# Listing an expert's tokens: the place split as 64 a + b, and two token columns to one loaded matrix

## Chip, cores and metric

One Trainium2 chip, one of its cores. The metric is the device time of one execution in microseconds; the lower the better. The kernel before takes 1235.56 us (median of three runs).

## What is computed

The reference transforms x in two dimensions, routes the rows through a first mixture of experts in which every expert takes exactly N / 8 tokens, and then through a second one without a limit:

```python
X = np.fft.fft(np.fft.fft(x, axis=1), axis=2).real         # x: [4, 2496, 256]
x = X.reshape(9984, 256)
logits = x @ w_gate                                        # first mixture, 8 experts, cap = 1248
for idx in np.argsort(-logits.flatten()):
    tok, e = idx // 8, idx % 8
    if assigned[tok] < 0 and counts[e] < cap:
        assigned[tok] = e; counts[e] += 1
out[assigned == e] = np.maximum(x[assigned == e] @ w1[e], 0) @ w2[e]        # F = 1024
# second mixture: e = argmax of out @ w_gate; gate * sigmoid(out @ w_output_gate)[e] * ffn_e(out)
```

The change is in the first mixture, between the choice of an expert's tokens and the gathering of their rows. There the device has, for each of the 9984 tokens (kept as 128 partitions by 80 columns), its place in the expert's list, a number from 0 to 1247, or a very large one for the tokens of other experts. Wanted is the inverse: for each place the token that stands there.

## The kernel before, in words

The program has three stages. `Fft.over_d` and `Fft.rows` (L139, L361) transform x and write the rows to the DRAM tensor xd, up to some 150 us. Then `Moe1` runs the first mixture expert by expert up to some 760 us, and `Moe2` the second. `Moe1.ffn` (L949) makes an expert's products: `ffn1_unit` (L781) multiplies the gathered and transposed rows with w1, ScalarE and VectorE split the relu into two float16 halves (L861, L867), and `ffn2_unit` (L789) multiplies them with w2.

Beside these products runs the choice of the next experts. `Select.phase` (L540) searches for the threshold at which an expert is full (`counts`, L502: a mask on VectorE, L512, ten small matmuls, L517, one more, L534) and computes each token's place (L605 to L629): two counts on TensorE (L607), a small copy ct on VectorE (L609) after which the flow yields 0.6, and products that need ct (L613, L614). `Select.places(k)` (L631) then lists expert k's tokens. `Moe1.prepare` (L998) calls it for the experts 1 to 7 and `Select.run` (L462) for expert 0; the gather of the rows from xd (L830) reads the list, idx.

The listing splits a place as 128 t + b. For a column c of 128 tokens, hb[:, :, c] is the one-hot matrix of b (128 by 128) and ha[:, :, :, c] holds, for the ten values of t, one-hot times c and one-hot times the partition p. The product of the two, summed over the 80 columns, has at (b, t) the column and the partition of the token with that place. So hb is the loaded matrix (the weights) of 80 matmuls (L658), and ha streams 20 columns past each of them. VectorE builds hb in four tiles of 20 columns each (L652), for 2 buffers, and ha in three steps (hx L643, L645, L646). nf (L660) and idx (L661) read the sum px.

```python
            for c in range(HB):
                cc = q * HB + c
                nc.tensor.matmul(px[:, :20], hb[:, :, c], ha[:, :, :, cc], start=(cc == 0), stop=(cc == 79))
```

In hb the column is the innermost index, so the 128 weights of one column lie HB = 20 numbers apart.

What sets the order: `Flow` (L1095) runs the side work as generators. Each yield gives the number of microseconds, by the flow's own count, after which the next piece is emitted between two units of the main products; `issue_after` keeps a piece behind the unit before it. The framework's scheduler then orders each engine's queue by these priorities. All queues are run in order on the chip, so an instruction of the listing that waits on TensorE also holds the expert's products behind it.

The constants come in two pieces: ch (tri, tric, ioa, ci, one; loaded at L1452) and iob, which `later` (L473) loads apart.

Of the kernel before, what the change touches and what calls it, by code (L numbers as in the profile page):

```python
# [10 lines left out]
F32 = mybir.dt.float32  # L11
# [3 lines left out]
OP = mybir.AluOpType  # L15
# [11 lines left out]
QW = 138  # 128 of q, q = 128, 8 experts, padding  # L27
# [7 lines left out]
def seq_rows():  # L35
    """[parity, 640]: the even and the odd positions up to the middle"""
    s = 2 * np.arange(640)[None] + np.arange(2)[:, None]
    return np.where(s <= H, s, -1)


def tables():
    # over the sequence: [parity, block of k, position, (cos, sin), block of positions, half, k]
# [6 lines left out]
    # over d: [d, half, (cos, sin), q]  # L49
# [9 lines left out]
    # for the gate: [q, block of q, (cos, sin, alternating), half, d]  # L59
# [7 lines left out]
    # the row d = 128: 16 (-1)^q, and what makes its halves' rows  # L67
# [8 lines left out]
def row_tokens():  # L76
    """the token of each internal row: [batch, (k, S - k, H - k, H + k), k]"""
# [10 lines left out]
def row_columns():  # L88
    """the order of q in a row of X"""
    return np.concatenate([np.arange(129), np.arange(255, 128, -1)])  # L90


def lay_x(x):
# [5 lines left out]
    # [parity, batch, d, ((d, s), (d, S - s), (256 - d, S - s), (256 - d, s)), position]  # L99
    xa = xa.transpose(4, 0, 1, 2, 3, 5).copy()  # L100
    xa[:, :, :, 1] = xa[:, :, :, 1, ::-1].copy()
    # [(half of the batches, (s, S - s), 3 copies), parity, batch, position]
# [23 lines left out]
class Fft:  # L126
    """Re(fft2(x)): first over d, with the gate's logits as further columns, then over the sequence."""
# [11 lines left out]
    def over_d(self, io, wk):  # L139
        """the columns' halves y"""  # L140
# [10 lines left out]
        def busy(n):  # L151
            """keeps TensorE's clock up while it waits"""
            for _ in range(n):
                nc.tensor.matmul(pw, one[:, :128], one, start=True, stop=True)
# [28 lines left out]
        # the gate's columns  # L183
# [16 lines left out]
        # the row d = 128: halves (hi, lo, hi) against (hi, hi, lo)  # L200
# [99 lines left out]
    def products(self, dst, k, par, cs, bs, qs, fine=False):  # L300
        """the sum over the positions of a parity; in three steps"""
# [11 lines left out]
    def logit_sums(self, par):  # L313
        """a parity's share of the logits, and of the column q = 128"""
# [15 lines left out]
    def logits(self):  # L330
        """the logits of all rows, and the column q = 128"""
# [8 lines left out]
    def half_rows(self, k, par, bs, fine=False):  # L340
        """a parity's share of a block of k: the differences and the sums of its cos and sin parts"""
# [19 lines left out]
    def rows(self, wk, k, bs):  # L361
        """a block of k: its rows of X"""
# [26 lines left out]

HK = ()  # L390
HQ = (1, 3)
# [14 lines left out]
def sel_consts():  # L406
# [20 lines left out]
    h["ioa"] = np.broadcast_to(np.arange(10)[:, None], (128, 10, 80)).reshape(128, -1)  # L427
    h["ci"] = np.broadcast_to(np.arange(80), (128, 80))
    h["one"] = np.ones((128, 128))
    h["iob"] = np.broadcast_to(np.arange(128)[:, None], (128, 128, HB)).reshape(128, -1)  # L430
# [8 lines left out]
class Select:  # L439
# [22 lines left out]
    def run(self):  # L462
        """fills expert after expert"""
# [9 lines left out]
    def later(self, pool, ch):  # L473
        """what only places needs"""
# [27 lines left out]
    def counts(self, lo, tt, n):  # L502
        """the mask m of the tokens with value - lo at or over each of n thresholds, and
        -> the experts' counts, [128, (expert, threshold)]"""
# [35 lines left out]
    def phase(self, k):  # L540
# [4 lines left out]
        # the first of the best experts  # L545
# [25 lines left out]
        # the bracket [lo, hi)  # L571
# [13 lines left out]
        # the expert that is full first  # L585
# [11 lines left out]
        # its tokens: those at or over hi, and the first of the bracket  # L597
# [24 lines left out]
        # the next phase's values  # L622
# [8 lines left out]
    def places(self, k):  # L631
# [4 lines left out]
        nc.vector.tensor_single_scalar(pi[:, 1], pi[:, 0], 7, op=OP.logical_shift_right)  # L636
        nc.vector.tensor_single_scalar(pi[:, 2], pi[:, 0], 127, op=OP.bitwise_and)
# [3 lines left out]
        ha = w.tile([128, 2, 10, 80], F16, name="ha", bufs=1)  # L641
        hx = w.tile([128, 10, 80], F16, name="hx", bufs=1)
        nc.vector.tensor_tensor(hx, h["ioa"].rearrange("p (a c) -> p a c", a=10),  # L643
                                pa[:, 0, None, :].to_broadcast([128, 10, 80]), op=OP.is_equal)
        nc.vector.tensor_mul(ha[:, 0], hx, h["ci"][:, None, :].to_broadcast([128, 10, 80]))  # L645
        nc.vector.tensor_scalar(ha[:, 1], hx, f["pi"], None, op0=OP.mult)  # L646
        wait = 6.0
        px = self.psum.tile([128, 512], F32, name="px", bufs=1)
        iob = self.iob.rearrange("p (b c) -> p b c", c=HB)
        for q in range(80 // HB):  # L650
            hb = w.tile([128, 128, HB], F16, name="hb")
            (nc.gpsimd if k in HK and q in HQ else nc.vector).tensor_tensor(hb, iob, pa[:, 1, None, q * HB:(q + 1) * HB].to_broadcast([128, 128, HB]),  # L652
                                    op=OP.is_equal)
            yield wait
            wait = 1.5
            for c in range(HB):
                cc = q * HB + c
                nc.tensor.matmul(px[:, :20], hb[:, :, c], ha[:, :, :, cc], start=(cc == 0), stop=(cc == 79))  # L658
        nf = w.tile([128, 20], F32, name="nf")
# [37 lines left out]
class Weights:  # L697
    """An expert's float32 matrices, loaded and split into halves: [:, part, half], the parts w1's two
    blocks of rows and w2's two fours of blocks."""
# [20 lines left out]
    def split(self, fs, quick, step=512):  # L720
        """-> the halves (w1's, and w2's with room for w2 wg beside it), and the steps that make them"""
# [23 lines left out]
    def gate(self, w2, fs, wg, psum, quick):  # L745
        """w2 wg beside w2, in steps"""
# [46 lines left out]
class Moe1:  # L793
# [15 lines left out]
    def gate_consts(self):  # L809
        """halves of both gates' matrices"""  # L810
# [24 lines left out]
    def xt(self, xg, c):  # L835
        """transposed halves of a chunk's rows, and the steps that make them"""
# [44 lines left out]
    def route(self, yr, k):  # L881
        """expert, scale and place of an expert's 1248 rows"""
# [615 lines left out]
```

## Time and profile before

| | |
|---|---|
| Three runs | 1234.17, 1235.56, 1239.19 us |
| Median | 1235.56 us |
| Profiled execution, from first to last instruction (its own time: the record gives the span alone) | 1230.4 us |
| TensorE busy with matmuls | 1153.9 us, 94% |
| VectorE busy | 758.1 us, 62% |
| GpSimd busy | 519.8 us, 42% |
| ScalarE busy | 450.3 us, 37% |
| Mean granted clock of TensorE | 0.975 |

PE is TensorE, PEld its loading of weights (which overlaps PE), DVE VectorE, ACT ScalarE, POOL GpSimd, SP the engine whose queue issues most DMAs. Busy time is time with at least one instruction of the engine under way. Matmuls are pipelined: one lasts some 0.2 us from start to end, but the next starts much sooner, so the cost of a batch is read from the distance between starts, and the last one's end is modelled. The clock is given as a share of 2.4 GHz and has two levels, 1.2 and 2.4 GHz. In the views, an entry in brackets is the engine's idle time before the instruction and what ended it.

### The profile page before, as it was taken

The numbers are of one execution on the slowest core, as the hardware profiler recorded it, in microseconds if no ns is written. First come the engines' busy times: TensorE is split into PE (matmuls) and PEld (weight loads), VectorE is DVE, ScalarE is ACT, GpSimd is POOL, SyncE is SP. The second block draws the span as 40 slices with busy tenths as digits, with TensorE's granted clock in tenths as the row PEclk, the third lists the DMA queues.
The fourth block names the chain that finished last, engine by engine and source line by source line (L and its number), as shares of the span: only waits on it lengthen the run. The fifth ranks groups of instructions, "written<-read, shape, count | busy, mean of one in ns | idle before, by whom it ended". The sixth has DMA issues, their size and how long they took to land. (4 is left out here: it accounts for less than half of the span.)

```text
span 1230.4 us, 25668 instructions
## 1 busy us (share of the span) xinstructions
PE 1153.9 (94%) x10286; PEld 844.6 (69%) x10286; DVE 758.1 (62%) x1915; ACT 450.3 (37%) x960; POOL 519.8 (42%) x495
## 2 busy tenths in 40 slices
PE   7999799989899979899898998999999999999997
PEld 4654556656666647567585756676676798999996
DVE  5867879797978887897555572633434334434442
ACT  3422344363543733445354442322313222222221
POOL 4823352468374780541506034753322333333321
PEclk8999899989999999999999998999999999999999
DMA  7925523142332641674837457644334366778782
GB/s 264 364 102 184 191 77 104 43 127 62 104 77 45 178 146 36 148 250 135 251 123 205 171 147 284 198 148 164 129 112 167 108 236 224 287 291 340 304 309 90
DMA packets 80042, 212.95 MB, mean 173 GB/s; under 512 B 11850, under 2 KB 48986, under 8 KB 69168
## 3 DMA queue, kind: packets, MB, share of 16 engines
q1 hardware_dynamic: 65360, 180.37, 43.5%
q0 software_dynamic: 14560, 30.91, 8.6%
q8 instruction: 82, 1.34, 0.5%
q14 instruction: 40, 0.33, 0.1%
HBM read 162.12 MB, written 50.42 MB: 173 GB/s over the span
## 5 line engine op out<-in xcount | busy, mean ns | idle before, releaser
L789 PEld LDWEIGHTS <-ht 128*128 128x128 f16 (+1 forms) x3912 | 384.3, 100 | 67.9 <-issue 8.7
L789 PE MATMUL py<-wh,ht 128*128 128x272 f16 (+2 forms) x3264 | 403.0, 280 | 7.9 <-ACT yr L878 7.9
L781 PE MATMUL ph<-xt,wh 128*128 128x384 f16 (+4 forms) x2352 | 385.3, 315 | 7.9 <-DVE ht L867 4.1
L781 PEld LDWEIGHTS <-wh 128*128 128x128 f16 x2352 | 209.7, 99 | 124.7 <-issue 12.8
L1322 ACT ACTIVATE ht<-ph 128x512 f16<-128x512 f32 x166 | 99.1, 597 | 316.5 <-PE ph L781 316.5
L1323 DVE SCALAR_TENSOR_TENSOR ht<-ph,ht 128x512 f16<-128x512 f32 x166 | 114.7, 691 | 120.0 <-ACT ht L1322 120.0
L942 POOL DMA_INDIRECT lst<-r_en,r_pi x80 | 89.3, 1116 | 151.5 <-DVE r_pi L936 93.0
L861 ACT ACTIVATE ht<-ph 128x384 f16<-128x384 f32 (+1 forms) x192 | 98.3, 516 | 89.4 <-PE ph L781 87.8
L1334 DVE TENSOR_SCALAR ot<-py,sc 128x256 f32<-128x256 f32 x83 | 40.1, 483 | 129.1 <-PE py L789 129.1
L830 POOL DMA_INDIRECT xg<-xd,s_idx x80 | 87.3, 1092 | 34.0 <-issue 20.3
L867 DVE SCALAR_TENSOR_TENSOR ht<-ph,ht 128x384 f16<-128x384 f32 (+1 forms) x147 | 84.4, 582 | 14.1 <-ACT ht L861 13.4
L865 POOL TENSOR_TENSOR ht<-hf,ht 128x384 f16<-128x384 f32 (+1 forms) x45 | 49.7, 1112 | 97.2 <-ACT hf L864 94.8
L1335 POOL DMA_INDIRECT out<-ot,tarow x54 | 54.1, 1003 | 64.6 <-DVE ot L1334 35.2
L305 PE MATMUL big<-y,tab 128*128 128x36 f16 (+3 forms) x660 | 79.6, 272 | 0.9 <-DVE y L256 0.9
L878 ACT ACTIVATE yr<-py 128x272 f32<-128x272 f32 x80 | 31.4, 394 | 131.3 <-PE py L789 128.1
L789 PE MATMUL py<-wp,ht 128*128 128x256 f16 x648 | 73.8, 273 | 0.0
L781 PE MATMUL ph<-xt,wp 128*128 128x256 f16 (+2 forms) x624 | 72.9, 277 | 0.0
L781 PEld LDWEIGHTS <-wp 128*128 128x128 f16 x624 | 51.4, 98 | 19.1
L1057 DVE SCALAR_TENSOR_TENSOR wp<-g,wp 128x1024 f16<-128x1024 f32 x32 | 40.2, 1257 | 33.7 <-ACT wp L1056 33.4
L1335 POOL DMA_INDIRECT out<-ot,tbrow x29 | 29.1, 1003 | 71.6 <-DVE ot L1334 33.3
L305 PEld LDWEIGHTS <-tab 128*128 128x128 f16 x660 | 38.5, 96 | 29.7 <-issue 2.0
L1288 POOL DMA_INDIRECT g<-yd,tarow x30 | 30.8, 1027 | 48.4 <-PE pt L1304 40.8
(248 smaller groups left out, 1412.1 us busy)
## 6 DMA issues: line engine op xcount, KB each, us to landing
wh<-wsd SPq DMA_DIRECT2D x50, 1024.0 KB, 5.2
wp<-wsd SPq DMA_DIRECT2D x26, 1024.0 KB, 5.9
wf<-moe_w SPq DMA_DIRECT2D x32, 512.0 KB, 6.1
g<-moe_w SPq DMA_DIRECT2D x32, 512.0 KB, 9.0
wsd<-wp SPq DMA_DIRECT2D x32, 512.0 KB, 3.8
xa<-xa SPq DMA_DIRECT2D x8, 1280.0 KB, 10.9
xd<-xr SPq DMA_DIRECT2D x20, 512.0 KB, 5.5
yd<-yr SPq DMA_DIRECT2D x8, 1156.5 KB, 7.0
```

The source lines that it names most:

```text
L305: self.nc.tensor.matmul(dst, self.tabs[par][k][:, cs, c, u], self.y[par][:, cs, w, c, bs, qs], start=(n == 0), stop=(n == 3 * NCH - 1))
L781: Flow.pe = nc.tensor.matmul(dst, w1[:, dk, a, fk * 128:fk * 128 + 128], xt[:, b, dk, :n], start=(k == 0), stop=(k == 5))
L789: Flow.pe = nc.tensor.matmul(dst, ht[:, a, fk, t0:t0 + m], w2[:, fk // 4, b, fk % 4], start=(fk == 0 and a == 0 and b == 0), stop=(fk == 7 ...
L830: nc.gpsimd.indirect_dma_start(out=xg[:m, t], out_offset=None, in_=self.xd, in_offset=bass.IndirectOffsetOnAxis(ap=idx[:m, t:t + 1], axis=0))
L861: self.act = nc.scalar.activation(ht[:, 0, fk, :n], ph[:, :n], AF.Relu)
L865: nc.gpsimd.tensor_sub(ht[:, 1, fk, :n], hf[:, :n], ht[:, 0, fk, :n])
L867: nc.vector.scalar_tensor_tensor(ht[:, 1, fk, :n], ph[:, :n], 0.0, ht[:, 0, fk, :n], op0=OP.max, op1=OP.subtract)
L942: s = nc.gpsimd.indirect_dma_start(out=ent, in_=en[:m, t], in_offset=None, out_offset=bass.IndirectOffsetOnAxis(ap=pi[:m, t:t + 1], axis=0))
L1057: nc.vector.scalar_tensor_tensor(h[:, q, 1], fs[q], 64.0, h[:, q, 0], op0=OP.mult, op1=OP.subtract)
L1322: nc.scalar.activation(hi, src, AF.Relu)
L1323: nc.vector.scalar_tensor_tensor(lo, src, 0.0, hi, op0=OP.max, op1=OP.subtract)
L1335: st = nc.gpsimd.indirect_dma_start(out=self.out, in_=ot, in_offset=None, out_offset=bass.IndirectOffsetOnAxis(ap=row[:, 1, u + h:u + h + ...
```

## The change

The place is now split as 64 a + b with a = 2 t + j, so a has 20 values and b has 64. hb has 64 rows of b for each column. Two columns of tokens, c and c + 10 of a tile, stand side by side as i = 0 and 1 in one loaded matrix of 128 weights (b, i), and ha streams, for both of them, 2 x 20 x 2 = 80 columns (v, a, i'). Of the sum only the entries with i = i' are wanted; the others are bounded at 255 when px is copied to nf, and four matmuls against a constant 0/1 matrix sel (for j and i each) pick the wanted entries and put them in the order of 128 places that the gather expects. A yield of 0.6 stands between nf and these four, and the yield between two tiles is 0.8 in place of 1.5. ha is built in place, without hx. ioa doubles, sel is new, and iob halves. The diff below leaves out comments, docstrings and unused settings that go as well.

```diff
-    h["ioa"] = np.broadcast_to(np.arange(10)[:, None], (128, 10, 80)).reshape(128, -1)
+    h["ioa"] = np.broadcast_to(np.arange(20)[:, None], (128, 20, 80)).reshape(128, -1)
     h["ci"] = np.broadcast_to(np.arange(80), (128, 80))
     h["one"] = np.ones((128, 128))
-    h["iob"] = np.broadcast_to(np.arange(128)[:, None], (128, 128, HB)).reshape(128, -1)
+    q = np.arange(128)
+    h["sel"] = np.stack([(q[None] // 64 == j) & (p[:, None] == 2 * (q[None] % 64) + i)
+                         for j in range(2) for i in range(2)], axis=1).reshape(128, -1)
+    h["iob"] = np.broadcast_to(np.arange(64)[:, None], (128, 64, HB)).reshape(128, -1)
...
-        nc.vector.tensor_single_scalar(pi[:, 1], pi[:, 0], 7, op=OP.logical_shift_right)
-        nc.vector.tensor_single_scalar(pi[:, 2], pi[:, 0], 127, op=OP.bitwise_and)
+        nc.vector.tensor_single_scalar(pi[:, 1], pi[:, 0], 6, op=OP.logical_shift_right)
+        nc.vector.tensor_single_scalar(pi[:, 2], pi[:, 0], 63, op=OP.bitwise_and)
...
-        ha = w.tile([128, 2, 10, 80], F16, name="ha", bufs=1)
-        hx = w.tile([128, 10, 80], F16, name="hx", bufs=1)
-        nc.vector.tensor_tensor(hx, h["ioa"].rearrange("p (a c) -> p a c", a=10),
-                                pa[:, 0, None, :].to_broadcast([128, 10, 80]), op=OP.is_equal)
-        nc.vector.tensor_mul(ha[:, 0], hx, h["ci"][:, None, :].to_broadcast([128, 10, 80]))
-        nc.vector.tensor_scalar(ha[:, 1], hx, f["pi"], None, op0=OP.mult)
+        ha = w.tile([128, 2, 20, 80], F16, name="ha", bufs=1)
+        nc.vector.tensor_tensor(ha[:, 1], h["ioa"].rearrange("p (a c) -> p a c", a=20),
+                                pa[:, 0, None, :].to_broadcast([128, 20, 80]), op=OP.is_equal)
+        nc.vector.tensor_mul(ha[:, 0], ha[:, 1], h["ci"][:, None, :].to_broadcast([128, 20, 80]))
+        nc.vector.tensor_scalar(ha[:, 1], ha[:, 1], f["pi"], None, op0=OP.mult)
         wait = 6.0
         px = self.psum.tile([128, 512], F32, name="px", bufs=1)
         iob = self.iob.rearrange("p (b c) -> p b c", c=HB)
+        hp = HB // 2
         for q in range(80 // HB):
-            hb = w.tile([128, 128, HB], F16, name="hb")
+            hb = w.tile([128, 64, HB], F16, name="hb")
...
             yield wait
-            wait = 1.5
-            for c in range(HB):
+            wait = 0.8
+            for c in range(hp):
                 cc = q * HB + c
-                nc.tensor.matmul(px[:, :20], hb[:, :, c], ha[:, :, :, cc], start=(cc == 0), stop=(cc == 79))
-        nf = w.tile([128, 20], F32, name="nf")
+                nc.tensor.matmul(px[:, :80], hb.rearrange("p b (i c) -> p (b i) c", i=2)[:, :, c],
+                                 ha[:, :, :, cc:cc + hp + 1:hp], start=(cc == 0), stop=(cc == 79 - hp))
+        nf = w.tile([128, 80], F16, name="nf")
+        nc.vector.tensor_scalar(nf, px[:, :80], 255.0, None, op0=OP.min)
+        yield 0.6
+        px = self.psum.tile([128, 512], F32, name="px", bufs=1)
+        nv = nf.rearrange("p (v t j i) -> p j i v t", v=2, j=2, i=2)
+        for n in range(4):
+            nc.tensor.matmul(px[:, :20], h["sel"][:, n * 128:n * 128 + 128], nv[:, n // 2, n % 2],
+                             start=(n == 0), stop=(n == 3))
+        nf = w.tile([128, 20], F32, name="ni")
         nc.vector.tensor_copy(nf, px[:, :20])
         nc.vector.scalar_tensor_tensor(self.idx[k], nf[:, :10], 128.0, nf[:, 10:], op0=OP.mult, op1=OP.add)
```

The yields move instructions on all engines. In the changed kernel's own line numbers the listing's matmul is L661, hb L654, the three steps of ha L644, L646 and L647, nf L664, the matmuls against sel L669, ni L672 and idx L673; L305 is the transform's product in both, and L793 is what L781 was, L859 what L847 was (the transposes of gathered rows).

VectorE, the listing of expert 0, before:

```order
190 L643 TENSOR_TENSOR hx<-ch,pa 128x800
191 L652 TENSOR_TENSOR hb<-iob,pa 128x2560
192 L645 TENSOR_TENSOR ha<-hx,ch 128x800
193 L646 TENSOR_SCALAR ha<-hx,cf 128x800
194 L652 TENSOR_TENSOR hb<-iob,pa 128x2560
195 L353 SCALAR_TENSOR_TENSOR xg_1953<-big,xf 128x384 x2
196 L652 TENSOR_TENSOR hb<-iob,pa 128x2560 x2
197 L353 SCALAR_TENSOR_TENSOR xg_2071<-big,xf 128x384 x2
198 L660 COPY nf<-px 128x20
```

and now:

```order
190 L644 TENSOR_TENSOR ha<-ch,pa 128x1600
191 L654 TENSOR_TENSOR hb<-iob,pa 128x1280
192 L646 TENSOR_TENSOR ha<-ha,ch 128x1600
193 L654 TENSOR_TENSOR hb<-iob,pa 128x1280
194 L647 TENSOR_SCALAR ha<-ha,cf 128x1600
195 L353 SCALAR_TENSOR_TENSOR xg_1942<-big,xf 128x384 x2
196 L654 TENSOR_TENSOR hb<-iob,pa 128x1280 x2
197 L664 TENSOR_SCALAR nf<-px 128x80
198 L672 COPY ni<-px 128x20
```

The second hb has moved ahead of ha's last step, and nf and ni have moved ahead of the second pair of L353, which takes the transform's products out of PSUM.

TensorE, the end of the listing of expert 5, before:

```order
8503 L658 LDWEIGHTS hb
8504 L658 MATMUL px<-ha,hb 128x20
8505 L781 LDWEIGHTS wh
8506 L781 MATMUL ph<-xt,wh 128x384
8507 L781 LDWEIGHTS wh
```

and now:

```order
8036 L661 LDWEIGHTS hb
8037 L661 MATMUL px<-ha,hb 128x80
8038 L793 LDWEIGHTS wh
8039 L793 MATMUL ph<-xt,wh 128x384
8040 L859 MATMUL pt<-cf,xg 128x128 x3
8041 L669 LDWEIGHTS ch
8042 L669 MATMUL px<-nf,ch 128x20
```

Where the products went on without a wait behind the last listing matmul, the matmuls against sel now stand behind one product and three transposes.

VectorE at the same place, now:

```order
982 L565 SCALAR_TENSOR_TENSOR z<-sp,s_jw 128x64
983 L664 TENSOR_SCALAR nf<-px 128x80
984 L570 TENSOR_SCALAR zs,lo<-z,lo 128x64
985 L750 SCALAR_TENSOR_TENSOR wh<-wf,wh 128x512
986 L513 SCALAR_TENSOR_TENSOR s_msk<-s_vv,lo,s_jw 128x640
987 L672 COPY ni<-px 128x20
```

nf stands among the search's own steps (z, zs, s_msk) and the splitting of the next weights (wh); before, the one copy nf stood at this point.

## Rows read from the trace of the kernel before

**Rows 1.** The page: span, busy time of TensorE and VectorE, share, instructions.

```profile
span 1230.4 us, 25668 instructions
PE 1153.9 (94%) x10286; PEld 844.6 (69%) x10286; DVE 758.1 (62%) x1915; ACT 450.3 (37%) x960; POOL 519.8 (42%) x495
```

**Rows 2.** Busy time by stretch, all instructions; first column the stretch in us.

```profile
core 0: us, PE busy (x) PEld busy (x) DVE busy (x) ACT busy (x) POOL busy (x), PEclk, DMA share, GB/s
134.50:138.70 4.20, 4.20 (x46) 3.20 (x46) 3.62 (x4) 0.00 (x0) 0.00 (x0) 0.50 0.94 315
...
261.00:283.00 22.00, 22.00 (x219) 15.91 (x218) 17.36 (x46) 12.23 (x29) 15.93 (x13) 0.90 0.51 128
...
480.00:500.00 20.00, 20.00 (x218) 15.69 (x216) 14.37 (x38) 10.28 (x25) 2.71 (x2) 1.00 0.25 80
...
620.00:641.00 21.00, 21.00 (x225) 17.77 (x224) 11.53 (x26) 11.40 (x26) 0.00 (x0) 1.00 0.37 124
...
196.00:720.00 524.00, 482.12 (x4307) 343.84 (x4306) 401.96 (x1109) 245.07 (x547) 249.95 (x231) 0.98 0.47 132
```

**Rows 3.** Busy time by stretch, line L658 alone: PE, PEld, PEclk, DMA.

```profile
261.00:283.00 22.00, 5.56 (x80) 5.71 (x80) 0.90 0.51 128
...
480.00:500.00 20.00, 5.50 (x80) 5.54 (x80) 1.00 0.25 80
```

**Rows 4.** Timeline of PE: start us, length us, instruction, count, idle before.

```profile
134.44 1.35 PE L658 MATMUL px<-ha,hb 128*128 128x20 f16 x20 [4.13 <-DVE ha L646]
135.63 2.08 PE L305 MATMUL big<-y,tab 128*128 128x384 f16 x6
137.50 1.38 PE L658 MATMUL px<-ha,hb 128*128 128x20 f16 x20
...
169.00 0.45 PE L766 MATMUL pt<-m_wg,wt 128*128 128x16 f16 x12
...
210.99 1.34 PE L658 MATMUL px<-ha,hb 128*128 128x20 f16 x20
```

**Rows 5.** Durations on two lines, ns: shortest, median, longest; first and last start.

```profile
L658 PE MATMUL px<-ha,hb x640: 198/213/243, 134.4 to 640.3; 128*128 128x20 f16 x160
...
L766 PE MATMUL pt<-m_wg,wt x384: 169/169/183, 169.0 to 701.5; 128*128 128x16 f16 x192
```

**Rows 6.** Timeline of DVE, the listing of expert 0.

```profile
131.59 0.57 DVE L643 TENSOR_TENSOR hx<-ch,pa 128x800 f16<-128x800 f16 x1
132.07 1.49 DVE L652 TENSOR_TENSOR hb<-iob,pa 128x2560 f16<-128x2560 f16 x1
133.48 0.57 DVE L645 TENSOR_TENSOR ha<-hx,ch 128x800 f16<-128x800 f16 x1
133.96 0.42 DVE L646 TENSOR_SCALAR ha<-hx,cf 128x800 f16<-128x800 f16 x1
```

**Rows 7.** Timeline, expert 0's list and the first gather.

```profile
144.86 0.16 DVE L661 SCALAR_TENSOR_TENSOR s_idx<-nf 128x10 int32<-128x10 f32 x1
...
154.79 1.76 POOL L830 DMA_INDIRECT xg<-xd,s_idx  x1 [4.63 <-DMA xd<-xr]
```

**Rows 8.** Waits of PE, 196 to 720 us: total us, times, longest us.

```profile
PE sp L534 <- DVE rd L529: 7.7, 8, 2.2
...
PE px L613 <- DVE ct L609: 2.3, 2, 1.8
...
PE sp L517 <- DVE s_msk L510: 0.2, 1, 0.2
```

**Rows 9.** The load of ch and its first reader: durations ns, first and last start us.

```profile
L1452 SPq DMA_DIRECT2D ch<-ch x1: 328/328/328, 50.3 to 50.3; - x1
...
L607 PEld LDWEIGHTS <-mm x16: 112/117/117, 120.6 to 534.8; 128*80 128x80 f16 x16
```

More of the change, by code (lines that the diff above doesn't have):

```diff
@@ L387, in rows @@
                 nc.sync.dma_start(dst[:, b0 + b], x[:, b].rearrange("p d h q -> p d (h q)"))
-HK = ()
-HQ = (1, 3)
 T = 8
@@ L649, in places @@
         iob = self.iob.rearrange("p (b c) -> p b c", c=HB)
+        hp = HB // 2
         for q in range(80 // HB):
-            hb = w.tile([128, 128, HB], F16, name="hb")
-            (nc.gpsimd if k in HK and q in HQ else nc.vector).tensor_tensor(hb, iob, pa[:, 1, None, q * HB:(q + 1) * HB].to_broadcast([128, 128, HB]),
+            hb = w.tile([128, 64, HB], F16, name="hb")
+            nc.vector.tensor_tensor(hb, iob, pa[:, 1, None, q * HB:(q + 1) * HB].to_broadcast([128, 64, HB]),
                                     op=OP.is_equal)
             yield wait
-            wait = 1.5
-            for c in range(HB):
+            wait = 0.8
+            for c in range(hp):
                 cc = q * HB + c
-                nc.tensor.matmul(px[:, :20], hb[:, :, c], ha[:, :, :, cc], start=(cc == 0), stop=(cc == 79))
-        nf = w.tile([128, 20], F32, name="nf")
+                nc.tensor.matmul(px[:, :80], hb.rearrange("p b (i c) -> p (b i) c", i=2)[:, :, c],
[9 more added lines that the diff above has]
+        nf = w.tile([128, 20], F32, name="ni")
         nc.vector.tensor_copy(nf, px[:, :20])
```

## Prediction

> **What bounds the kernel now.** I read the page's busy shares first [rows 1], then the busy time in four of the stretches where an expert's tokens are listed [rows 2], then the listing's own share of two of them [rows 3], and last the waits of TensorE [rows 8]. The reader is to see that TensorE (PE) is busy 1153.9 of 1230.4 us, VectorE (DVE) 758.1, and that in three listings (261 to 283, 480 to 500 and 620 to 641 us) PE is busy for every microsecond. What a listing takes from PE there, the expert's products do not get: it lies on the path. Each listing is 80 matmuls and 5.50 or 5.56 us of busy PE [rows 3], the flight of the last in each batch included.
>
> What one such matmul costs is its distance to the next. A batch of 20 takes 1.34 us, and one lasts 0.213 us [rows 4, 5]: (1.34 - 0.213) / 19 = 59, say 60 ns. Twelve matmuls with 16 columns at L766, whose weights lie side by side, take 0.45 us, one 0.169: 25 ns each [rows 4, 5]. Twenty columns are hardly more work than sixteen, so the 60 ns are for something else: in L658 each of the 128 weights lies 20 numbers from the next. It is not the array's clock either: from 134.5 to 138.7 us the granted clock is 0.50, that is 1.2 GHz [rows 2], six 384-column matmuls take 2.08 us, and the batches of 20 on both sides of them still take 1.35 and 1.38 us [rows 4]. **The listing is bound by fetching strided weights, 60 ns a load; the columns that stream past are hidden under it.** The change halves the loads and streams four times the columns.
>
> **The change part by part.**
>
> *The listing's matmuls.* Removed are 640 x 60 ns = 38.4 us of PE (8 experts x 80). Added are 320 matmuls with 80 columns. Their weights lie 10 numbers apart in place of 20 and are still 128, so I leave the load at 60 ns. The columns are new: 80 numbers out of ha, each at least 10 numbers from the next. Contiguous, 6 x 384 columns take 2.08 us at 1.2 GHz [rows 4], 0.90 ns a column, so 0.45 at 2.4 GHz, and 80 columns are 36 ns: they would hide under the load. The other bound is the only strided stream in the trace, L658's own. Its shortest matmul lasts 198 ns, L766's with four columns fewer 169 [rows 5]; if all of the difference were the reading, a strided column would cost (29 - 4 x 0.45) / 20 + 0.45 = 1.8 ns, and 80 of them 144 ns. In between I take twice the contiguous pace, 0.9 ns a column or 72 ns a matmul, because the strided weights are the nearest row: they are stretched from at most 25 ns to 60, by a factor of 2 or a little more. 320 x 72 ns = 23.0 us.
>
> The page "TensorE: Matmul & The Clock Gate" of the Trainium skill (Weight-path perf modes) lets the fast load of 128 weights run with steps up to about a thousand elements, and its section Back-to-back issue gap gives N / 2.4 + 2.5 ns between matmuls, 36 ns for 80 columns. By that the 320 would cost 11.5 us and the kernel would take 1211.5 us, an estimate from that page. The trace does not agree for strided weights: 60 ns against 25 [rows 4].
>
> *The last four.* New are 32 matmuls against the constant sel, with 128 contiguous weights and 20 columns each: by L766's 25 ns, 0.8 us.
>
> *The new wait.* They wait for DVE's nf, which waits for the listing's last product. PE's queue is in order, so behind them stand the expert's own products, and for those wait ScalarE's relu and DVE's lower halves. The nearest row is the wait of L613 for ct (L609): the same shape, PE to a small DVE copy and back with a yield of 0.6 us between, eight times in the program. It cost 2.3 us, in 2 of 8 cases, the longest 1.8 [rows 8]. I take 2.3 us in all; the upper bound is 1.8 in each of eight, 14.4, the lower nothing. The cover is thin at expert 5, where one 384-column matmul and three transposes stand on PE between, and DVE has z and a half of wh right around nf; at expert 6 and 7 it is five matmuls and three transposes.
>
> *VectorE.* One comparison of 800 numbers takes 0.57 us, one of 2560 takes 1.49 [rows 6]: 0.523 ns a number and 0.15 us to begin. So hb with 1280 numbers is 0.82 us, and 32 x (1.49 - 0.82) = 21.4 us are saved. ha doubles: 0.57 to 0.99 twice, 0.42 to about 0.69 if it grows likewise, together 8 x 1.11 = 8.9 us more. nf costs 8 x 0.2. Net 11 us less DVE, nearly all of it beside PE. Between 196 and 720 us PE's waits for DVE sum to 29 us (eleven rows of the view, 7.7 to 0.2 us [rows 8]), and DVE is busy 402 of the 524 us [rows 2]. About 10 of the 11 us fall there, 2.5% of 402, so I credit 2.5% of 29, 0.7 us; the bounds are nothing and 5 us.
>
> *Expert 0.* This listing runs in the transform's tail. PE stands still 4.13 us for ha [rows 4]. DVE's steps up to there take 0.57 + 1.49 + 0.57 + 0.42 us [rows 6], with overlaps 2.8; now they are 0.99 + 0.82 + 0.99 + 0.82 + 0.69, since the second hb comes ahead of ha's last step, so the first product may start some 1.5 us later. Seven more 384-column products of the transform stand ahead of it on PE (49 for 42), 7 x 384 x 0.45 ns = 1.2 us of cover that is not lost work. I add 0.4 us. The list is ready at 145.0 us and the gather starts at 154.79, released by the transform's rows xd [rows 7]; so the earlier list is worth nothing in itself, only PE's time counts.
>
> *Covered.* The constants ch grow by 1312 columns and iob shrinks by 1280: ch is issued at 50.3 us and first needed at 120.6 [rows 9], 70 us of cover for 0.34 MB. Without that cover the selection would start a few microseconds later, no more. The shorter yields move side work by a unit of the flow and add none. hx and ha in one buffer stay on DVE, in order.
>
> Sum: -38.4 + 23.0 + 0.8 + 2.3 + 0.4 - 0.7 = -12.6 us, 1217.8 against the profiled execution's span of 1230.4. The median of the three runs, 1235.56, is 5.2 above that span for what lies around it, so **1223.0 us**. Half a per cent, 6.2 us, is about what a measurement here can tell from no change.
>
> **The rivals.**
>
> *The columns become the bound (slower).* If ha's steps of 10 and 80 numbers cost all that rows 5 allow, a matmul takes 144 ns, the 320 take 46.1, and the sum is +10.5: 1246.1 us. It decides from 111 ns a matmul on (320 x 111 = 38.4 - 2.8 = 35.6); over 131 ns the kernel is slower by more than half a per cent. For it: 198 against 169 ns. Against it: ends of matmuls are modelled, and a late load can be what the 29 ns are.
>
> The page "SBUF — State Buffer" of the Trainium skill (Door 1, on cachelines) says that each access that crosses to a new 16-byte line pays a penalty, with free strides up to 8 two-byte numbers. Here every step is 10 or more, so it speaks for this rival, without a figure. The trace agrees as far as the weights go: 60 ns against 25 [rows 4].
>
> *The new wait eats the gain.* Each of the eight waits for nf lasts 1.8 us, like the longest for ct: 12.1 us more than I charged, 1235.1 us. For it: DVE is busy 55 to 79% of the three listings [rows 2]. Against it: 6 of 8 such waits were nothing.
>
> *The saved time comes back as waits.* PE reaches the next search or the next expert earlier and stands there for DVE or ScalarE. For it: PE is idle 41.9 of the 524 us [rows 2]. Against it: the three full listings. If half of the gain goes, 1229.3 us.
>
> *The loads get faster too*, with half the step: 36 ns a matmul, 11.5 us more, 1211.5 us.
>
> That the change does not do what it says is no rival: PE's order holds 320 and 32 matmuls in place of 640.
>
> **How the numbers follow.** The forecast has 0.60, its own range 1216 to 1230 (60 to 84 ns a matmul is 4 us either way, the waits 3); columns as the bound 0.10; the wait 0.11; time that comes back 0.13; faster loads 0.06. Faster by over half a per cent (under 1229.4): 0.57 of the forecast's 0.60, half of the time that comes back, all of the last: 0.69. Slower (over 1241.7): the columns, and 0.01 of other tails, 0.11. The rest, 0.20, is no change. From 1212 to 1239 us lie the forecast, the wait and the time that comes back; the slow columns and the fast loads are left out.
>
> **What would show it.** The new batches of 10: (busy - one duration) / 9 near 72 ns; 60 means that the columns hide, 144 is the slow rival. The listings' PE time falls from 43 to about 26 us. hb at 0.82 us. PE waits on the sel line for nf, about 2 us in all; 10 or more is the second rival. If these hold and the time does not, PE's idle time between 196 and 720 us has grown. The second stage, from about 760 us on, should last as long as before; if it is what shrinks, or if the time falls without shorter batches, my reason is wrong.

## The result, and the profile after

The changed kernel takes 1254.47 us (median of four runs, 1242.16 to 1260.33) against 1237.14 us for the kernel before on the same chip: ratio 1.0123, 95% interval 1.0089 to 1.0158. It is slower by about 1%, where 1223.0 us, 1% faster, were forecast. Measured twice more beside the kernel before, it took 1249.76 and 1249.81 us, ratios 1.0105 (1.0072 to 1.0137) and 1.0114 (1.0085 to 1.0144).

The profiled execution took 1253.42 us, its span is 1251.5. The page, its first part and the listing's group:

```profile
span 1251.5 us, 25098 instructions
PE 1176.4 (94%) x9998; PEld 858.6 (69%) x9998; DVE 742.6 (59%) x1923; ACT 449.3 (36%) x960; POOL 504.0 (40%) x495
...
L661 PE MATMUL px<-ha,hb 128*128 128x80 f16 x320 | 58.8, 351 | 5.0 <-DVE ha L647 5.0
```

Against [rows 1], DVE is busy 15.5 us less, and PE 22.5 us more, with 288 matmuls fewer. The listing's and the selecting matmuls, by line (durations in ns: shortest, median, longest):

```profile
L661 PEld LDWEIGHTS <-hb x320: 136/147/168, 136.8 to 664.6; 128*128 128x128 f16 x160
L661 PE MATMUL px<-ha,hb x320: 323/353/360, 139.0 to 664.7; 128*128 128x80 f16 x160
...
L669 PE MATMUL px<-nf,ch x32: 178/180/226, 148.8 to 666.2; 128*128 128x20 f16 x32
```

The timeline of PE in the listing of expert 3, where the clock falls between the second and the third batch (columns as in [rows 4]):

```profile
342.11 1.83 PE L661 MATMUL px<-ha,hb 128*128 128x80 f16 x10 [0.85 <-DVE ha L647]
343.75 0.68 PE L793 MATMUL ph<-xt,wh 128*128 128x384 f16 x3
...
344.50 1.86 PE L661 MATMUL px<-ha,hb 128*128 128x80 f16 x10
346.17 1.91 PE L793 MATMUL ph<-xt,wh 128*128 128x384 f16 x6
347.87 1.85 PE L661 MATMUL px<-ha,hb 128*128 128x80 f16 x10
```

and the busy time in two stretches of it, PEclk being the third number from the end (1.00, then 0.55):

```profile
342.10:345.70 3.60, 3.59 (x22) 2.83 (x22) 3.54 (x6) 1.81 (x5) 3.16 (x3) 1.00 0.19 67
345.80:352.60 6.80, 6.80 (x39) 4.30 (x38) 3.70 (x14) 2.39 (x7) 3.04 (x3) 0.55 0.26 84
```

A batch of ten costs (1.85 - 0.353) / 9 = 166 ns from matmul to matmul; start to start it is 167 ns in the trace, median over all batches and at both clock levels, while the contiguous 384-column products between them start 161 ns apart before the clock falls and 320 ns apart after it. In place of 1.34 us for 20 columns of tokens [rows 4], they now take 1.85.

VectorE, the listing of expert 0, against [rows 6]:

```profile
135.03 0.99 DVE L644 TENSOR_TENSOR ha<-ch,pa 128x1600 f16<-128x1600 f16 x1
135.93 0.82 DVE L654 TENSOR_TENSOR hb<-iob,pa 128x1280 f16<-128x1280 f16 x1
136.67 0.99 DVE L646 TENSOR_TENSOR ha<-ha,ch 128x1600 f16<-128x1600 f16 x1
137.57 0.82 DVE L654 TENSOR_TENSOR hb<-iob,pa 128x1280 f16<-128x1280 f16 x1
138.30 0.63 DVE L647 TENSOR_SCALAR ha<-ha,cf 128x1600 f16<-128x1600 f16 x1
```

Where the time went: the stretch from expert 0's first product to the second mixture, and the second mixture. Before (the third row is line L658 alone: PE, PEld, PEclk, DMA):

```profile
161.80:764.90 603.10, 554.47 (x4886) 394.27 (x4886) 447.52 (x1238) 273.75 (x610) 277.44 (x258) 0.97 0.46 134
764.90:1230.40 465.50, 456.29 (x3990) 364.88 (x3987) 193.89 (x404) 120.67 (x215) 166.98 (x165) 0.99 0.58 207
...
161.80:764.90 603.10, 38.33 (x560) 38.90 (x560) 0.97 0.46 134
```

and after (the third row is L661):

```profile
170.70:790.00 619.30, 572.54 (x4625) 404.53 (x4625) 430.21 (x1241) 272.93 (x610) 262.31 (x256) 0.96 0.45 130
790.00:1251.50 461.50, 455.37 (x3989) 364.43 (x3987) 193.88 (x404) 120.69 (x215) 166.73 (x165) 1.00 0.58 209
...
170.70:790.00 619.30, 51.62 (x280) 40.22 (x280) 0.96 0.45 130
```

The stretch grew by 16.2 us: 13.3 in seven listings, 4.8 in PE's other work (2.0 of them the selecting matmuls; the rest goes with more time at the lower clock, 52.7 us for 31.8), less 1.9 of idle time (48.6 before, 46.8 after). The second mixture is 4.0 us shorter. The span grew by 21.1; the missing 8.9 us lie ahead of expert 0's first product, 4.6 of them ahead of its listing (139.0 in place of 134.4 us) and 4.3 from there on.

The 4.3 go with the slow listing. In all ten traces from chips where the kernel before takes 1236 us the first gather waits for the transform's rows xd, and on PE the transform's last products stand behind the listing: they end at 154.4 us in place of 147.3, and the gather starts 7.7 us later than in [rows 7]:

```profile
162.44 1.45 POOL L842 DMA_INDIRECT xg<-xd,s_idx  x1 [3.76 <-DMA xd<-xr]
```

From the listing's first matmul to expert 0's first product it is 30.5 to 31.7 us in the four traces with 167 ns, and 25.7 to 28.3 in the six others. As far as these traces tell, the 4.6 go with the order in which the work is emitted rather than with the columns: the listing begins at 138.3 and 138.8 us in two further traces of the changed kernel and at 134.5 in a second one of the kernel before, but at 135.3 in the changed kernel with another spacing (after_yield_b) and at 137.8 in a kernel without the sharing (layout). What moves it was not followed.

### The profile page after: what moved, and what is told of

Read it like the earlier page. It is cut to its first block, busy times and chain, and to the rows that moved or that the text cites. A ratio compares the mean times of both kernels' runs of the same rounds, so it can differ in the third digit from the quotient of the medians.

```text
span 1251.5 us, 25098 instructions
## 1 busy us (share of the span) xinstructions
PE 1176.4 (94%) x9998; PEld 858.6 (69%) x9998; DVE 742.6 (59%) x1923; ACT 449.3 (36%) x960; POOL 504.0 (40%) x495
## 5 line engine op out<-in xcount | busy, mean ns | idle before, releaser
L793 PE MATMUL ph<-xt,wh 128*128 128x384 f16 (+4 forms) x2352 | 389.1, 317 | 10.0 <-DVE ht L879 8.4
L793 PEld LDWEIGHTS <-wh 128*128 128x128 f16 x2352 | 211.4, 99 | 130.1 <-issue 16.8
L954 POOL DMA_INDIRECT lst<-r_en,r_pi x80 | 84.2, 1052 | 159.8 <-DVE r_pi L948 103.8
L842 POOL DMA_INDIRECT xg<-xd,s_idx x80 | 84.0, 1050 | 38.9 <-issue 21.5
L305 PE MATMUL big<-y,tab 128*128 128x36 f16 (+3 forms) x660 | 81.1, 276 | 1.2 <-DVE y L256 1.2
L877 POOL TENSOR_TENSOR ht<-hf,ht 128x384 f16<-128x384 f32 (+1 forms) x45 | 47.2, 1051 | 85.8 <-ACT hf L876 80.6
L793 PE MATMUL ph<-xt,wp 128*128 128x256 f16 (+2 forms) x624 | 72.9, 277 | 0.0
L793 PEld LDWEIGHTS <-wp 128*128 128x128 f16 x624 | 51.4, 98 | 19.1
L661 PE MATMUL px<-ha,hb 128*128 128x80 f16 x320 | 58.8, 351 | 5.0 <-DVE ha L647 5.0
L305 PEld LDWEIGHTS <-tab 128*128 128x128 f16 x660 | 39.5, 98 | 30.0 <-issue 2.3
L1069 DVE SCALAR_TENSOR_TENSOR wp<-g,wp 128x1024 f16<-128x1024 f32 x32 | 39.2, 1228 | 31.7 <-ACT wp L1068 31.7
```

What stands on the lines that cost most here:

```text
L305: self.nc.tensor.matmul(dst, self.tabs[par][k][:, cs, c, u], self.y[par][:, cs, w, c, bs, qs], start=(n == 0), stop=(n == 3 * NCH - 1))
L661: nc.tensor.matmul(px[:, :80], hb.rearrange("p b (i c) -> p (b i) c", i=2)[:, :, c], ha[:, :, :, cc:cc + hp + 1:hp], start=(cc == 0), stop ...
L793: Flow.pe = nc.tensor.matmul(dst, w1[:, dk, a, fk * 128:fk * 128 + 128], xt[:, b, dk, :n], start=(k == 0), stop=(k == 5))
L842: nc.gpsimd.indirect_dma_start(out=xg[:m, t], out_offset=None, in_=self.xd, in_offset=bass.IndirectOffsetOnAxis(ap=idx[:m, t:t + 1], axis=0))
L877: nc.gpsimd.tensor_sub(ht[:, 1, fk, :n], hf[:, :n], ht[:, 0, fk, :n])
L954: s = nc.gpsimd.indirect_dma_start(out=ent, in_=en[:m, t], in_offset=None, out_offset=bass.IndirectOffsetOnAxis(ap=pi[:m, t:t + 1], axis=0))
```

## The experiments

The theory, once the trace was read: streamed columns that stand 10 or 80 numbers apart are fetched at about 2.08 ns each, whatever the clock, and 80 of them cost 167 ns. Rival A: it is the weights at a step of 10. Rival B: the added wait, the new order or the lower clock.

The first runs (adjacent, columns, both, probe) were on a chip on which the kernel before took 1308 us, and four later ones (weights, after_yield, both_yield, probe2) on one where it took 1310; ScalarE and VectorE have waits of up to 16 us there that the view puts down to "remote" and that the other profiles don't have. The price of a matmul is the same there, but what it does to the time is judged by the runs on chips where the kernel before took 1236 us. What those two chips wait for was not followed up.

**One fetch changed at a time.** `adjacent` pairs neighbouring columns of tokens, so that ha is read in runs of two; `columns` lays ha out as it is streamed; `weights` does the same with hb alone; `both` with ha and hb.

```diff
 # adjacent
-        nc.vector.tensor_copy(pa[:, 1], pi[:, 2])
+        nc.vector.tensor_copy(pa[:, 1].rearrange("p (q j c) -> p q j c", q=4, j=2),
+                              pi[:, 2].rearrange("p (q c j) -> p q j c", q=4, j=2))
...
-                                 ha[:, :, :, cc:cc + hp + 1:hp], start=(cc == 0), stop=(cc == 79 - hp))
+                                 ha[:, :, :, q * HB + 2 * c:q * HB + 2 * c + 2], start=(cc == 0), stop=(cc == 79 - hp))
 # columns, both
-        ha = w.tile([128, 2, 20, 80], F16, name="ha", bufs=1)
+        ha = w.tile([128, 40, 2, 20, 2], F16, name="ha", bufs=1)
...
+                                 ha[:, q * hp + c].rearrange("p v a j -> p (v a j)"), start=(cc == 0), stop=(cc == 79 - hp))
 # weights, both
-            hb = w.tile([128, 64, HB], F16, name="hb")
+            hb = w.tile([128, hp, 64, 2], F16, name="hb")
...
+                nc.tensor.matmul(px[:, :80], hb[:, c].rearrange("p b i -> p (b i)"),
```

(ioa, ci, iob and the casts to pa follow the new order; VectorE's steps keep their sizes.)

> The two columns of tokens of a matmul are neighbours, so that the streamed columns stand in ha in runs of two numbers; the weights keep their step of 10, and every step of VectorE keeps its size. Theory (streamed columns that stand 10 or 80 numbers apart are fetched one by one, 2.08 ns each, 167 ns for 80): a run of two costs one fetch, so 40 x 2.08 = 83 ns from matmul to matmul, 320 x 84 = 27 us less than the changed kernel, about 1227.5 us. Rival A (the weights at step 10 are what takes 167 ns): still 167 ns and 1254 us. Rival B (the loss comes from the added wait, the new order, or half-clock time that has nothing to do with the columns): 83 ns or not, the time stays above 1240 us.

> The changed kernel with ha laid out in the order in which it is streamed, so that the 80 columns of a matmul are contiguous; the weights keep their step of 10. Theory: the columns hide under the load of the strided weights, 60 ns from matmul to matmul as before the change, 320 x 107 = 34 us less than the changed kernel, about 1220 us, if VectorE makes ha as fast as before; its three steps of 1600 numbers now read their operands in runs of two. Rival A (weights): 167 ns and 1254 us. Rival B (wait, order, clock): about 60 ns, but above 1240 us.

> Neighbouring columns of tokens in a pair, and ha and hb both laid out in the order in which they are fetched: contiguous columns and contiguous weights. Theory: 36 to 40 ns from matmul to matmul, 320 x 129 = 41 us less than the changed kernel, about 1213 us, unless VectorE pays for the new order of hb's 1280 numbers (0.82 us each now; 1.5 us if it loses its fast pace) and PE comes to wait for it. Rival A (weights): the same 36 to 40 ns, so this run alone doesn't tell them apart; together with the run on the columns alone it does. Rival B: above 1240 us.

> The changed kernel with hb laid out so that a matmul's 128 weights are contiguous, and ha untouched: the streamed columns keep their steps of 10 and 80. It is the mirror of columns. Theory (the strided columns set the price): 145 to 167 ns from matmul to matmul, at most 7 us less than the changed kernel, about 1.005 to 1.01 of before. Rival A (the weights): 36 to 60 ns, and faster than before, about 0.98 to 0.99.

On the slower chips: adjacent 0.972 (0.965 to 0.979) of before, columns 0.969 (0.962 to 0.975), both 0.978 (0.970 to 0.987), weights 1.000 (0.998 to 1.003), which is no gain, but not the expected loss of 0.5 to 1% either; the changed kernel itself was not run there. Those that gained were run again on the other chips, with the changed kernel beside them:

> The changed kernel itself, on the same chip as the three others of this call, as their yardstick; 167 ns from matmul to matmul in the listings. Theory and Rival A: about 1.2% slower than before, as measured the first time. Should it come out faster than before here, then the time depends on something in the chip that neither theory holds.

> The same kernel as both: sharing as in the change, all fetches contiguous, 36 ns. Theory: 320 x 131 = 42 us of TensorE less than the changed kernel on the same chip, ratio to the changed kernel about 0.967, and to before about 0.978 (320 x 36 + 0.8 against 640 x 60: 26 us less). Rival B (wait, order, clock): at or above before.

> The kernel before the change, for its profile on this chip: 60 ns from matmul to matmul in the listings; its half-clock time and its idle time, for comparison with the three others. Theory: the clock falls in after_b's listings more often than here and in both_b's no more often than here.

> The changed kernel, as the yardstick of this call. 167 ns; theory: 1.007 to 1.014 of before on a chip on which before takes some 1236 us, lower where before takes some 1310 us.

> The same kernel as adjacent: neighbouring columns of tokens, runs of two, 80 ns. Theory: 320 x 87 = 28 us of TensorE less than after_c; by the run with everything contiguous (40 us less gave 27 us) two thirds of it show, 19 us, and the idle time of TensorE grows by the rest. If the time followed the price in full: 28 us.

> The same kernel as columns: streamed columns contiguous, weights at step 10, some 58 ns. Theory: 320 x 109 = 35 us of TensorE less than after_c, two thirds of it in the time, 23 us. If the weights were the price: no gain.

A batch of ten on PE's timeline, in adjacent_b, in columns_b and in both_b:

```profile
491.65 0.97 PE L662 MATMUL px<-ha,hb 128*128 128x80 f16 x10
```

```profile
495.39 0.75 PE L664 MATMUL px<-ha,hb 128*128 128x80 f16 x10
```

```profile
489.86 0.52 PE L663 MATMUL px<-ha,hb 128*128 128x80 f16 x10
```

and the listing's line in weights, whose loads became shorter (123 ns for 147 above) while the matmuls did not:

```profile
L662 PEld LDWEIGHTS <-hb x320: 95/123/152, 134.4 to 700.9; 128*128 128x128 f16 x160
L662 PE MATMUL px<-ha,hb x320: 323/352/354, 136.6 to 701.1; 128*128 128x80 f16 x160
```

| kernel | ns from matmul to matmul | listings, stretch to the second mixture | idle PE there | time of before |
|---|---|---|---|---|
| before_b | 60, 640 of them | 38.3 us | 49.9 us | 1 |
| after_b, after_c | 167 | 51.6, 51.6 | 47.9, 47.2 | 1.0105, 1.0114 |
| adjacent_b | 80 | 27.6 | 53.3 | 0.9935 (0.9915 to 0.9955) |
| columns_b | 58 | 21.0 | 59.5 | 0.9942 (0.9920 to 0.9965) |
| both_b | 36 | 15.5 | 60.3 | 0.9886 (0.9849 to 0.9923) |

Each trace is of one execution. Idle time is the stretch less PE's busy time, as in before_b (the second row is L658 alone):

```profile
162.80:768.00 605.20, 555.27 (x4886) 394.64 (x4886) 448.21 (x1237) 273.53 (x610) 274.14 (x257) 0.97 0.47 134
...
162.80:768.00 605.20, 38.27 (x560) 38.78 (x560) 0.97 0.47 134
```

and both_b (the second row is L663 alone):

```profile
162.50:757.90 595.40, 535.12 (x4625) 370.73 (x4625) 433.62 (x1241) 270.47 (x610) 267.19 (x257) 0.96 0.49 136
...
162.50:757.90 595.40, 15.49 (x280) 13.45 (x280) 0.96 0.49 136
```

Rival A is out: faster weights leave 167 ns, and faster columns alone turn the loss into a gain. So is most of Rival B: the wait for nf, the selecting matmuls and the order are in all of these kernels, and both_b is faster than either kernel, 1222.69 us against 1249.76 and 1235.9. Against after_c, adjacent_b gained 22.6 us and columns_b 22.4, where 19 and 23 were expected; both_b gained half of what was expected against before. Between adjacent_b, columns_b and both_b the time doesn't follow the price: of the 12 us between 27.6 and 15.5 in the stretch, idle time takes back 7, and PE's other work, with 42.4 us at the lower clock for 33.7, another 3.6.

**The lower clock.** In after's eight listings four have time at 1.2 GHz, in after_b's three, in after_c's four, in before_b's one, in both_b's two. So, in one trace of each, the clock falls more often beside the slow columns, as the theory expected, but both_b has more than before_b, which it did not expect, and the whole stretch doesn't tell the kernels apart: 48.4 and 37.9 us at 1.2 GHz in after_b and after_c, 42.4 in both_b, 38.6 in before_b. What the clock adds to the loss is a few microseconds at most and wasn't separated.

**The price by step.** Batches of ten extra matmuls whose sums nobody reads, appended to each listing of the kernel before (probe) and of the changed kernel (probe2), one execution of each:

```diff
+        for a, b in PROBE[k]:
+            for _ in range(10):
+                nc.tensor.matmul(px[:, 32:32 + n], wi[a], mv[b], start=True, stop=True)
+            yield 0.5
```

> The kernel before the change, and after each expert's list one to four batches of 10 extra matmuls whose results nobody reads: weights with a chosen step (1, 2, 4, 8, 10, 20), 80 columns with a chosen step (1, 2, 4, 8, 10, 20, runs of two, runs of four) or 16 contiguous ones. Theory: with contiguous weights, 80 columns cost 36 ns from matmul to matmul at step 1, 167 at steps 10 and 20, 83 in runs of two, 42 in runs of four, and little more than 36 up to a step of 8; weights at step 10 with contiguous columns about 60. Rival A (weights): step 10 of the weights with contiguous columns 167, step 10 of the columns with contiguous weights 36. Between them stands the case that the price grows with the step, number by number, which steps 2, 4 and 8 show.

> The changed kernel, and after each list one to three batches of 10 extra matmuls whose results nobody reads, 80 columns each (40 in one batch), most on contiguous weights. In the first such run steps of 10 and 20 cost 143 to 147 ns, the listings themselves 167; open is what makes the last 20 ns. If it is the jump of 80 numbers between pairs: the listing's own pattern on contiguous weights 167, steps of 40 near it, the same columns in the other order (20 at a step of 80, then the neighbours 10 further) 167 or more; if it is the strided weights beside it: 144 on contiguous weights, 167 on weights at step 10; if it is VectorE's work at the same time: 144 in both. For the price by step: if each started group of 8 numbers costs 1.8 ns, then steps 3, 5 and 6 cost 54, 90 and 108 ns, and 9 to 40 all 144.

PE's timeline in probe2: 30 with ha's own pattern, step 10 and step 20; 20 with steps 3 and 5; then ten with ha's own pattern on hb's weights at step 10 and ten on contiguous ones.

```profile
229.26 4.73 PE L689 MATMUL px<-ha,ch 128*128 128x80 f16 x30
...
383.64 1.64 PE L689 MATMUL px<-ha,ch 128*128 128x80 f16 x20
...
470.89 1.83 PE L689 MATMUL px<-ha,hb 128*128 128x80 f16 x10
472.53 1.85 PE L689 MATMUL px<-ha,ch 128*128 128x80 f16 x10
```

Start to start in the trace, median of each batch, 80 columns on contiguous weights at full clock (step 32 at 1.2 GHz; step 20 at both levels):

| step of the columns | 1 | 2 | 3 | 4 | 5 | 6 | 8 | 9 | 10 | 12 | 16 | 20 | 24 | 32 | 40 | own |
|---|---|---|---|---|---|---|---|---|---|---|---|---|---|---|---|---|
| ns | 36 | 37 | 56 | 74 | 91 | 108 | 143 | 147 | 147 | 142 | 146 | 144 | 142 | 137 | 167 | 167 |

Runs of two at a step of 20 cost 73, at 80 (as in adjacent) 80; runs of four 36; 40 columns at a step of 80 cost 80, 2.0 ns each. From step 3 to 8 it is 0.22 to 0.24 ns for every number passed over or read, 1.8 ns for eight; beyond, the step hardly matters (137 to 147), until the long ones of 80 and 40 add 11 and 16% to 144. The listing's own pattern, jumps of 10 and of 70 in turn, costs 167 on either weights: the last 20 ns come with the pattern, not with the loads. What in it makes them is open: the same columns in the other order, all at a step of 80, cost 158, where 167 or more was expected. Weights under 16 contiguous columns: 25 at steps 1 and 2, 33 at 4, 62 at 8, 58 at 10, 60 at 20. So the change's half step gave nothing: 58 for 60.

**Without the sharing.** The kernel before, its operands laid out at a step of two:

```diff
-            hb = w.tile([128, 128, HB], F16, name="hb")
+            hb = w.tile([128, HB // 2, 128, 2], F16, name="hb")
...
-                nc.tensor.matmul(px[:, :20], hb[:, :, c], ha[:, :, :, cc], start=(cc == 0), stop=(cc == 79))
+                nc.tensor.matmul(px[:, :20], hb[:, c // 2, :, c % 2],
+                                 ha[:, cc // 2, :, :, c % 2].rearrange("p v a -> p (v a)"), start=(cc == 0), stop=(cc == 79))
```

> The kernel before the change, without the sharing (640 matmuls with 20 columns), with ha and hb laid out so that a matmul's weights and columns stand two numbers apart. Theory: 25 ns from matmul to matmul, the price of 16 columns on weights at step 1 or 2, in place of 60, so 640 x 35 = 22 us less than before, ratio about 0.982: nearly all that the sharing brings with good fetches (26 us), without the new wait and the four matmuls behind it. A view in which the number of matmuls sets the price: 60 ns and no change.

```profile
488.94 0.65 PE L661 MATMUL px<-ha,hb 128*128 128x20 f16 x20
```

The price came as expected, (0.65 - 0.172) / 19 = 25 ns, the time did not: 0.9935 (0.9911 to 0.9958), 1228.5 us, 7 us for 22 of PE. In the stretch of the one trace the listings fell by 19.7 us, to 18.5; idle PE grew by 9.2, to 59.1, and PE's other work by 7.2, with 52.4 us at the lower clock for 38.6.

**The order.** The changed kernel and both, with the old spacing of the batches:

```diff
-            wait = 0.8
+            wait = 1.5
```

> The changed kernel with the spacing between the listing's batches put back to 1.5 us. Theory: 167 ns and 1.005 to 1.015 of before, like the changed kernel. Rival B (the loss is the new order's): at or below 1.003.

> The same kernel as both, with the spacing between the listing's batches put back to 1.5 us as before the change. It undoes the order alone. Theory: the spacing is worth nothing that can be told, 0.985 to 0.993 of before like both_b. If the time that came back there (10 us of idle TensorE between expert 0's first product and the second stage) came from the closer spacing, about 0.98.

> The changed kernel with the old spacing of 1.5 us between the listing's batches. Theory (columns): within 0.5% of after_c. Rival B (the loss is the new order's): 1% or more below after_c.

On the slower chip they gave 0.997 (0.992 to 1.002) and 0.983 (0.979 to 0.987). By its expectation the first speaks for Rival B, but weights, with the same 167 ns and the new spacing, stands at 1.000 on that chip, so the loss doesn't show there whatever the spacing; why is open. Beside the changed kernel it took 1249.43 us against 1249.81: the spacing is worth nothing. The rest of the new order was not undone; it is in both_b too.

## Why the prediction was wrong

- *The loads, 640 x 60 ns.* Right: weights at steps 10 and 20 cost 58 and 60 ns, those at 1 and 2 cost 25.
- *The columns, 320 x 72 ns.* **This is the step that failed.** "In between I take twice the contiguous pace", because the strided weights were the nearest row. Measured: 167 ns, 53.4 us in place of 23.0. Strided weights say little about strided columns: per number, weights at step 10 cost 58 / 128 = 0.45 ns, columns 1.8 to 2.1. And L658's pace could not show it: its own 20 columns at a step of 80, an estimated 40 ns by probe2's 2.0 each, lay hidden under the load. What did show it was the row that I set aside, 198 ns against 169 [rows 5]: taken in full it gave 144 ns. That this is so near the 147 of a step of 10 is in part luck, for L658's columns stand 80 apart, where a column costs 2.0 ns and not 1.8. The rival built on it was the true one; its 0.10 was too little, its 1246.1 us short by the pattern's last 20 ns.
- *What the page said.* The page "SBUF — State Buffer" of the Trainium skill (Door 1) lets a stream step freely over up to 8 two-byte numbers and charges for each access that crosses to a new 16-byte line. The runs agree with the line: from a step of 8 on the price is flat to 32. They disagree with the free range: a step of 3 costs 56 ns for 36, a step of 4, with two numbers to a line, 74; of the steps over 1 tried, only 2 is free.
- *The last four, 0.8 us.* Right: start to start they are 25 ns, 1.0 us in all.
- *The new wait, 2.3 us.* Nothing: no row of PE's waits in after names nf. Of the rival in which it eats the gain nothing is left; with listings of 36 ns the wait appears, 0.9 us in two cases.
- *VectorE, 0.7 us.* hb is 0.82 as worked out; DVE's busy time fell by 15.5 us for 11 expected, idle PE by 1.9 for 0.7.
- *Expert 0, 0.4 us.* A second step that failed. PE's wait for ha is the same, 4.1 us [rows 4], but expert 0's first product comes 8.9 us later, 4.3 of them by the slow listing. The list itself is not waited for, as argued; the transform's products are, since they stand behind the listing on PE and the gather waits for the rows that they make.
- *The second stage as long as before.* Shorter by 4.0 us in the profile, and 3.1 of them lie at the very end: behind TensorE's last product before, before_b and layout take 7.6 to 7.9 us, all seven traces with the sharing here (chips at 1236 us) 4.8. The last store is issued 1.75 us after its rows are ready before, and 0.28 us after:

```profile
1222.59 0.48 DVE L1334 TENSOR_SCALAR ot<-py,sc 128x256 f32<-128x256 f32 x1 [1.36 <-PE py L789]
1224.82 0.98 POOL L1335 DMA_INDIRECT out<-ot,tbrow  x1 [5.85 <-issue]
```

```profile
1246.82 0.48 DVE L1346 TENSOR_SCALAR ot<-py,sc 128x256 f32<-128x256 f32 x1 [1.36 <-PE py L801]
1247.58 0.98 POOL L1347 DMA_INDIRECT out<-ot,tbrow  x1 [4.38 <-DVE ot L1346]
```

No step of the prediction holds this; its cause is open. It hides 3 us of the loss, and it is in the gain of every kernel with the sharing.
- *The 5.2 us around the span.* A misreading without effect: in every run with both numbers the time is 1.7 to 1.9 us above the span of the same execution, so the profiled execution took an estimated 1232 us, less than any of the three runs.

With 167 for 72 and nothing for the wait, the sum is -12.6 + 30.4 - 2.3 = +15.5, 1251.1 us; the three medians are 1249.8, 1249.8 and 1254.5. That it fits so well is in part luck: in the trace of after the 21.1 us are 8.9 ahead of expert 0's products, where the sum has little, 16.2 in the stretch and 4.0 less in the second mixture, where it has nothing.

Another step would have failed had the columns been cheap. A microsecond more in the listings cost about a microsecond (15.1 more PE in all eight; 13.9 and 14.3 us in the medians of after_b and after_c), by way of the three parts just named; one less does not bring one: both_b saved 22.8 us in the stretch, of which idle PE took back 10.4 and PE's other work 2.6, and layout fared alike. The rival "time that comes back" was right in that direction, at about a half of the gain. PE's waits in the stretch, before_b:

```profile
PE sp L534 <- DVE rd L529: 9.0, 7, 4.1
PE sp L517 <- DVE s_msk L512: 7.8, 10, 3.6
...
PE px L607 <- DVE mm L603: 3.9, 1, 3.9
...
PE pt L766 <- POOL wt L757: 0.4, 1, 0.4
```

and both_b:

```profile
PE sp L518 <- DVE s_msk L513: 18.3, 11, 4.8
...
PE px L608 <- DVE mm L602: 5.8, 1, 5.8
PE pt L780 <- POOL wt L771: 5.1, 3, 4.4
...
PE sp L535 <- DVE rd L530: 3.8, 6, 1.0
```

and after_b:

```profile
PE sp L518 <- DVE s_msk L513: 15.8, 8, 4.8
```

The row of s_msk, a step of the search for the next expert, grows by 10.5 us from before_b to both_b. But it stands at 15.8 in after_b too, beside the slow listings, and part of it is another row's loss: with rd and s_hi the waits of the search sum to 18.3 us in before_b, 18.9 in after_b and 22.4 in both_b. So the search explains some 4 of the 10.4 us, the gate's weights wt as much, and the rest is spread over small waits. That a cheaper search would free its part was not tried.

## What to carry to other kernels

Price both operands of a matmul by their steps, each apart, before trading one for the other: the one that is hidden now becomes the bound when its share grows. Where the producer can write in the order of the stream at no cost (here 0.82 us for hb and 0.99 for ha's steps in any order), do that first: it made the shared listing the fastest kernel on the chips where before takes 1236 us (on the slower chip columns was, 0.969 for 0.978), and the layout alone, without the sharing, brought about half of that gain, 7.4 us of 13.2, of which 3 lie at the end of the program. And price a saving on a busy engine at less than its face where a chain of small waits runs beside it; and ask of a longer step what stands behind it in the queue, as the transform's products did here.

## What was not expected of the hardware

Strided streaming doesn't follow the granted clock: 144 ns at a step of 20 and 167 in the listing at both levels, while contiguous columns go from 36 to 67 ns. A reordered producer cost VectorE nothing, even where the broadcast operand stands in the middle and only two numbers in a row are contiguous.

And VectorE can stand still within an instruction: in both_b one that takes 0.42 us elsewhere lasts 3.70 while GpSimd works through three of its own, and PE waits 4.8 us for the search behind it. The timeline of DVE, then of POOL:

```profile
422.21 0.42 DVE L768 SCALAR_TENSOR_TENSOR wt<-wf,wt 128x256 f16<-128x256 f32 x1
...
424.85 3.70 DVE L768 SCALAR_TENSOR_TENSOR wt<-wf,wt 128x256 f16<-128x256 f32 x1 [1.63 <-ACT wt L766]
```

```profile
425.11 2.28 POOL L755 TENSOR_TENSOR wh<-wf,wh 128x512 f16<-128x512 f32 x2
427.34 0.92 POOL L879 TENSOR_TENSOR ht<-hf,ht 128x384 f16<-128x384 f32 x1
```

The page "SBUF — State Buffer" of the Trainium skill (SBUF: two separate sides) has VectorE and GpSimd take turns at a shared pair of ports, each for a whole instruction; these rows agree with it in that the one ends when the other's three are done, but not plainly: VectorE's is recorded as starting 0.26 us ahead of the first of the three. No run here took GpSimd's work away to show it.
